# Wider weight transfers (2 MB, 14 to 16 KB rows) in a decode kernel: sliding-window attention with a gated FFN

## Chip, cores and metric

The kernel runs on one core of a Trainium2 chip. The metric is device time in microseconds (us), lower is better. Each execution reports its time and the mean clock that was granted to the TensorE. All runs counted here are fast: none lies more than 1.5% above the fastest of its kernel. In the profile PE is the TensorE matmul, PEld its weight load, DVE the VectorE, ACT the ScalarE, POOL the GpSimd, and SP the SyncE; an SPq entry is SP's sequencer, here the one that issues almost all DMAs.

## The reference

One decode step for 8 sequences with model width 512. A layer norm feeds two branches. Branch A is attention with 32 query heads over 8 cached K/V heads, of which only the last 1024 positions count. Branch B is a gated FFN of width 1792. The result combines them.

```python
x  = A_x                                    # (8, 1, 512), all bf16
xn = layernorm(x)
# A: q = xn @ wq -> 32 heads of 128; window of the last 1024 of 4096 positions
#    o = softmax(q k^T / sqrt(128)) v ;  s = o @ wo
# B: g = silu((gelu(xn @ w_gate) * (xn @ w_up)) @ w_down)
return x + s * g
```

K and V in the window are 33.6 MB. The weights wq, wo (4.19 MB each), w_gate, w_up and w_down (1.84 MB each) are 13.9 MB. Everything is read once: 47.46 MB.

## The kernel before

SP issues all large loads in the order of use, as 1 MB tiles (128 partitions of 8 KB) into one ring of 21 slots: K of the first group, four tiles of wq, then K and V of 16 groups alternating, six FFN tiles, four tiles of wo.

```python
ring = ctx.enter_context(tc.tile_pool(name="ring", bufs=21))
small = ctx.enter_context(tc.tile_pool(name="small", bufs=3))
def slot():
    return ring.tile([P, SLOT], BF16, name="slot")        # SLOT = 4096 elements, 8 KB
def load_wq():
    for k in range(NDC):                                   # 4 transfers of 1 MB
        t = slot()
        nc.sync.dma_start(out=t, in_=A_wq[k * P : (k + 1) * P, :])
        wq_t.append(t)
# ... load_ffn: two transfers of 896 KB, 7 KB rows, for each of gate, up, down
HS = SLOT // D                                             # 8 sub-rows of wo per partition
NM = Hq // HS                                              # 4 tiles of wo
def load_wo(m, cut=HS):
    t = slot().rearrange("p (e d) -> p e d", e=HS)
    src = A_wo[m * HS * Dh : (m + 1) * HS * Dh, :].rearrange("(p e) d -> p e d", e=HS)
    for lo, hi in ((0, cut), (cut, HS)):
        if lo < hi:
            nc.sync.dma_start(out=t[:, lo:hi, :], in_=src[:, lo:hi, :])
    wo_t[m] = t
# ...
for m in range(NM):
    load_wo(m, cut=HS if m < NM - 1 else HS - 2)           # last tile in two pieces
```

The output projection at the end is one group of matmuls per wo tile. A matmul waits for the transfer that brings the part it reads, so in the last tile 24 of the 32 matmuls wait for the piece of 6 sub-rows, and 8 wait for the last 2.

```python
def project_out(m):
    for e in range(HS):
        for q in range(NQ):                                # NQ = 4
            nc.tensor.matmul(s_ps[32 * q : 32 * q + B, :], oE[m][:, e, :],
                             wo_t[m][:, e, q * P : (q + 1) * P], ...)
# ... main loop over 64 blocks, then expand_out, ffn_up, select_out, ffn_down, then
for m in range(NM):
    project_out(m)
# tmp = s_ps * g ; out_sb = tmp + x ; four output writes, alternating SP and ACT
```

The softmax here doesn't subtract the row's maximum and nothing guards it: scores larger than these inputs give would overflow.

Of the kernel before, what the change touches and what calls it, by code (L numbers as in the profile page):

```python
# [10 lines left out]
BF16 = mybir.dt.bfloat16  # L11
# [4 lines left out]
def kernel(  # L16
# [13 lines left out]
    nc = tc.nc  # L30

    B, Sq, D = A_x.shape
# [5 lines left out]
    F = B_w_gate.shape[1]  # L38
    P = nc.NUM_PARTITIONS
    NDC = D // P  # L40
# [10 lines left out]
    CB = 8  # L51
    NB = C // CB
    SLOT = C * Dh

    JF = F // P
    NQ = D // P
# [3 lines left out]

    front = ctx.enter_context(tc.tile_pool(name="front", bufs=1))
    front.tile([P, 96], FP32, name="front_pad")
    ring = ctx.enter_context(tc.tile_pool(name="ring", bufs=21))
    consts = ctx.enter_context(tc.tile_pool(name="consts", bufs=1))
    persist = ctx.enter_context(tc.tile_pool(name="persist", bufs=1))
    kT_pool = ctx.enter_context(tc.tile_pool(name="kT_pool", bufs=4))
    p_pool = ctx.enter_context(tc.tile_pool(name="p_pool", bufs=3))
    small = ctx.enter_context(tc.tile_pool(name="small", bufs=3))
    ps_kT = ctx.enter_context(tc.tile_pool(name="ps_kT", bufs=3, space=bass.MemoryType.PSUM))
    ps_sc = ctx.enter_context(tc.tile_pool(name="ps_sc", bufs=2, space=bass.MemoryType.PSUM))  # L70
    ps_m = ctx.enter_context(tc.tile_pool(name="ps_m", bufs=2, space=bass.MemoryType.PSUM))
# [9 lines left out]
    def slot():  # L81
        return ring.tile([P, SLOT], BF16, name="slot")

    k_t, v_t, wo_t = {}, {}, {}
    wq_t, wg_t, wu_t, wd_t = [], [], [], []

    def load_cache(src, g):
        t = slot()
        hkv, b0 = g // GPH, (g % GPH) * I
        rows = src[b0 : b0 + I, hkv, win0:Sk, :].rearrange("i (r c) d -> r i (c d)", c=C)  # L90
        nc.sync.dma_start(out=t, in_=rows)  # L91
        return t
# [4 lines left out]
    def load_v(g):  # L97
        v_t[g] = load_cache(A_v_cache, g)

    def load_wq():  # L100
        for k in range(NDC):
            t = slot()
            nc.sync.dma_start(out=t, in_=A_wq[k * P : (k + 1) * P, :])  # L103
            wq_t.append(t)

    def load_ffn():
        for dst, src in ((wg_t, B_w_gate), (wu_t, B_w_up)):
            for a in range(2):
                t = slot()
                nc.sync.dma_start(  # L110
                    out=t[:, 0 : 2 * F],
                    in_=src[a * 2 * P : (a + 1) * 2 * P, :].rearrange(
                        "(p k) f -> p (k f)", k=2
                    ),
                )
                dst.append(t[:, 0 : 2 * F].rearrange("p (k f) -> p k f", k=2))
        JH = JF // 2
        wd = B_w_down.rearrange("(p j) d -> p j d", j=JF)
        for a in range(2):
            t = slot()[:, 0 : JH * D].rearrange("p (j d) -> p j d", j=JH)  # L120
            nc.sync.dma_start(out=t, in_=wd[:, a * JH : (a + 1) * JH, :])
            wd_t.extend(t[:, j, :] for j in range(JH))


    HS = SLOT // D
    NM = Hq // HS
    DQ = Dh // HS

    def load_wo(m, cut=HS):
        t = slot().rearrange("p (e d) -> p e d", e=HS)  # L130
        src = A_wo[m * HS * Dh : (m + 1) * HS * Dh, :].rearrange("(p e) d -> p e d", e=HS)
        for lo, hi in ((0, cut), (cut, HS)):
            if lo < hi:
                nc.sync.dma_start(out=t[:, lo:hi, :], in_=src[:, lo:hi, :])
        wo_t[m] = t

    load_k(0)
    load_wq()
    for g in range(1, NG):
        load_k(g)  # L140
        load_v(g - 1)
    load_v(NG - 1)
    load_ffn()
    for m in range(NM):
        load_wo(m, cut=HS if m < NM - 1 else HS - 2)


    ident = consts.tile([P, P], BF16, name="ident")
    nc.vector.memset(ident, 0.0)
    nc.gpsimd.affine_select(  # L150
        out=ident, in_=ident, compare_op=ALU.not_equal, fill=1.0, base=0,
# [10 lines left out]
        out=sel, in_=sel, compare_op=ALU.not_equal, fill=1.0, base=0,  # L162
# [4 lines left out]
        out=diag, in_=sel.rearrange("p r i -> p i r"), axis=AX.X, op=ALU.add  # L167
    )
    nc.vector.tensor_scalar(
        out=diag, in0=diag, scalar1=1.0, scalar2=30000.0, op0=ALU.subtract, op1=ALU.mult  # L170
# [6 lines left out]
        out=hmask, in_=hmask, compare_op=ALU.is_ge, fill=0.0, base=0,  # L177
# [3 lines left out]
        out=hmask, in_=hmask, compare_op=ALU.is_ge, fill=0.0, base=B - 1,  # L181
# [5 lines left out]
        out=bsel3, in_=bsel3, compare_op=ALU.not_equal, fill=1.0, base=0,  # L187
# [4 lines left out]
        out=bsel_f, in_=bsel3.rearrange("p h b -> p b h"), axis=AX.X, op=ALU.add  # L192
# [7 lines left out]
    for q in range(NQ):  # L200
        nc.scalar.dma_start(
            out=xq_sb[32 * q : 32 * q + B, :], in_=x_flat[:, q * P : (q + 1) * P]
# [10 lines left out]
    xhat = persist.tile([B, D], BF16, name="xhat")  # L213
    nc.vector.tensor_scalar(  # L214
        out=xhat, in0=x_sb, scalar1=mv[:, 0:1], scalar2=rstd[:, 0:1],
# [14 lines left out]

    def transpose_x():
        t = ps_m.tile([P, 2, NDC, B], BF16, name="m_ps")
        for k in range(NDC):
            nc.tensor.transpose(t[:, 0, k, :], xhat[:, k * P : (k + 1) * P], ident[0:B, 0:B])  # L234
        xp = xhat.rearrange("b (a p k) -> b a k p", a=2, k=2)
        for a in range(2):
            for k in range(2):
                nc.tensor.transpose(t[:, 1, 2 * a + k, :], xp[:, a, k, :], ident[0:B, 0:B])
        nc.vector.tensor_copy(out=xnT_sb[:, :, 0:B], in_=t[:, 0])
        nc.vector.tensor_copy(out=xpT_sb[:, :, 0:B], in_=t[:, 1])  # L240

# [153 lines left out]

    def ffn_up():
        gu_ps = [ps_m.tile([P, JQ * P], FP32, name="m_ps") for w in range(2)]
        for w, wt in enumerate((wg_t, wu_t)):
            for k in range(NDC):
                cols = wt[k // 2][:, k % 2, :].rearrange("x (p j) -> x j p", j=JF)  # L400
                for q in range(NQ):
                    nc.tensor.matmul(  # L402
                        gu_ps[w][Q * q : Q * (q + 1), :],
                        xpT_sb[:, k, :],
                        cols[:, j0[q] : j0[q] + JQ, :],
                        start=(k == 0),
                        stop=(k == NDC - 1),
                        skip_group_check=True,
                    )
        shape = [P, JQ * P]  # L410
        zT, uT = gu_ps
        z2 = persist.tile(shape, FP32, name="z2")
        nc.scalar.activation(out=z2, in_=zT, func=ACT.Square)
        nc.vector.tensor_scalar(
            out=z2, in0=z2, scalar1=0.044715, scalar2=1.0, op0=ALU.mult, op1=ALU.add
        )
        nc.vector.tensor_tensor(out=z2, in0=z2, in1=zT, op=ALU.mult)
        th = persist.tile(shape, FP32, name="th")
        nc.scalar.activation(out=th, in_=z2, func=ACT.Tanh, scale=0.7978845608028654)
        nc.vector.tensor_scalar(  # L420
            out=th, in0=th, scalar1=0.5, scalar2=0.5, op0=ALU.mult, op1=ALU.add
        )
        nc.vector.tensor_tensor(out=z2, in0=th, in1=zT, op=ALU.mult)
        h_sb = persist.tile(shape, BF16, name="h_sb")
        nc.vector.tensor_tensor(out=h_sb, in0=z2, in1=uT, op=ALU.mult)
        h_ps = ps_m.tile([P, JQ, P], BF16, name="m_ps")
        for c in range(JQ):
            nc.tensor.transpose(h_ps[:, c, :], h_sb[:, c * P : (c + 1) * P], ident)
        nc.vector.tensor_copy(out=hT_sb, in_=h_ps)

    def ffn_down():
        f_ps = ps_m.tile([P, P], FP32, name="m_ps")
        nc.vector.memset(f_ps, 0.0)
        for j in range(JF):
            r = j // JQ
            for q in range(NQ):
                nc.tensor.matmul(
                    f_ps[Q * q : Q * q + B, :],
                    hT_sb[:, j - j0[r], Q * r : Q * r + B],
                    wd_t[j][:, q * P : (q + 1) * P],  # L440
                    start=(j == 0),
                    stop=(j == JF - 1),
                    skip_group_check=True,
                )
        th2 = persist.tile([P, P], FP32, name="th2")
        nc.scalar.activation(out=th2, in_=f_ps, func=ACT.Tanh, scale=0.5)
        nc.vector.tensor_scalar(
            out=th2, in0=th2, scalar1=0.5, scalar2=0.5, op0=ALU.mult, op1=ALU.add
        )
        nc.vector.tensor_tensor(out=g_sb, in0=th2, in1=f_ps, op=ALU.mult)  # L450


    LA, LAG = 2, 6
    N = NG * NB
    transpose_x()
    for n in range(LA):
        transpose_block(n)
    project_q()
    for n in range(N + LAG):
# [4 lines left out]
        if n >= LAG:  # L464
# [3 lines left out]
            if g % GM == 0 and g > 0:  # L468
                if s == 0:
                    expand_out(g // GM - 1)  # L470
                if s == 3:
                    select_out(g // GM - 1)
    expand_out(NM - 1)
    ffn_up()
    select_out(NM - 1)
    ffn_down()
    xr_sb = persist.tile([P, P], FP32, name="xr_sb")
    nc.vector.tensor_copy(out=xr_sb, in_=xq_sb)
# [7 lines left out]
    for q in range(NQ):  # L486
        eng = nc.sync if q % 2 == 0 else nc.scalar
        eng.dma_start(
            out=out_flat[:, q * P : (q + 1) * P], in_=out_sb[32 * q : 32 * q + B, :]
# [31 lines left out]
```

## Time and profile before

| | before |
|---|---|
| time, median | 123.18 us (123.18 to 123.19, 3 runs) |
| span of the profile | 121.1 us |
| bytes read from HBM | 47.46 MB |
| share of queue 1 in the 16 DMA engines' span | 93.7% |
| PE / DVE / ACT busy | 71% / 60% / 19% |

The first lines are from the page of the kernel before: the slices (40 equal parts of the span, each 3.03 us; the DMA digit is the busy share in tenths), the DMA queue, and the chain of work that ended last.

```profile
DMA  3999999999999999999999999999999999999820
GB/s 84 387 430 430 430 427 417 419 430 425 425 427 427 425 414 422 430 419 430 425 427 422 422 417 430 422 425 422 425 433 418 422 414 434 416 430 423 341 88 5
DMA packets 6929, 47.73 MB, mean 394 GB/s; under 512 B 888, under 2 KB 896, under 8 KB 1920
q1 hardware_dynamic: 6800, 47.46, 93.7%
DMA 82%; PE 12%; DVE 2%; SPq 1%; issue 0%
```

The DMA is busy from the second slice to the 37th, at about 425 GB/s. No other engine is near that. So the time is the time to move 47.46 MB, plus what comes before the first byte and after the last.

What comes after the last bytes is in the timeline of the kernel before (start, duration, engine, line, operation, operands, count; in brackets the idle time before it and what ended it).

```profile
109.96 1.02 PE L383 MATMUL s_ps<-slot,oE_1066 128*8 128x128 bf16 x32 [0.32 <-DMA slot<-in_A_wo_dram]
112.40 1.02 PE L383 MATMUL s_ps<-slot,oE_1569 128*8 128x128 bf16 x32 [1.42 <-DMA slot<-in_A_wo_dram]
114.84 1.02 PE L383 MATMUL s_ps<-slot,oE_2072 128*8 128x128 bf16 x32 [1.42 <-DMA slot<-in_A_wo_dram]
116.75 1.02 PE L383 MATMUL s_ps<-slot,oE_2360 128*8 128x128 bf16 x32 [0.88 <-DMA slot<-in_A_wo_dram]
117.82 0.29 DVE L483 TENSOR_TENSOR tmp<-s_ps,g_sb 128x128 f32<-128x128 f32 x1 [7.06 <-PE s_ps L383]
118.47 0.71 SPq L488 DMA_DIRECT2D out_dram<-out_sb  x2
```

The wo tiles land every 2.44 us per 1 MB, which is 430 GB/s. The last group starts when the 768 KB piece has landed, at 116.75 us, and its 32 matmuls take 1.02 us; the remaining 256 KB lands under them. Then come two small DVE operations and the output writes.

### The profile page before, as it was taken

How to read it: one execution, taken by the hardware profiler on the slowest of the kernel's cores; microseconds unless marked ns; L12 is line 12 of the kernel's file. 1: busy time of each engine (PE TensorE's matmuls, PEld its weight loads, DVE VectorE, ACT ScalarE, POOL GpSimd, SP SyncE). 2: the span in 40 equal slices, each digit the busy share in tenths (PEclk: the TensorE clock that was granted, in tenths of full speed). 3: DMA queues.
4: the chain of work that ended last, by engine and by line, in shares of the span. 5: the costliest groups of instructions: out<-in, count | busy, mean ns of one | idle time of the engine just before them, and what ended most of it. 6: DMA issues, size and time to landing. Idle time of an engine off the chain costs nothing.

```text
span 121.1 us, 4123 instructions
## 1 busy us (share of the span) xinstructions
PE 86.0 (71%) x1856; PEld 71.1 (59%) x1856; DVE 72.3 (60%) x150; ACT 22.6 (19%) x70; POOL 2.4 (2%) x15
## 2 busy tenths in 40 slices
PE   0075269696875968999997969566798789955450
PEld 0061029586865957999896969565698542134340
DVE  2352046866956749678989987747798670562000
ACT  0440000321303301212330330303033300300000
POOL 6100000000000000000000000000000000000000
PEclk9999756999999985559999999999999756995555
DMA  3999999999999999999999999999999999999820
GB/s 84 387 430 430 430 427 417 419 430 425 425 427 427 425 414 422 430 419 430 425 427 422 422 417 430 422 425 422 425 433 418 422 414 434 416 430 423 341 88 5
DMA packets 6929, 47.73 MB, mean 394 GB/s; under 512 B 888, under 2 KB 896, under 8 KB 1920
## 3 DMA queue, kind: packets, MB, share of 16 engines
q1 hardware_dynamic: 6800, 47.46, 93.7%
q8 instruction: 14, 0.23, 0.7%
q10 hardware_dynamic: 112, 0.02, 0.1%
q14 instruction: 3, 0.02, 0.1%
HBM read 47.46 MB, written 0.01 MB: 392 GB/s over the span
## 4 chain that ended last, share of the span: by engine, by line
DMA 82%; PE 12%; DVE 2%; SPq 1%; issue 0%
DMA slot<-in_A_k_cache_dram 44%; DMA slot<-in_B_w_gate_dram 16%; DMA slot<-in_A_wo_dram 15%; DMA slot<-in_A_wq_dram 7%; PE kT_ps L282 7%; PE m_ps L329 2%; PE sc_ps L294 2%; SPq L91 1%; PE s_ps L383 1%; DVE kT L286 1%; PE m_ps L316 1%; DVE sums L318 1%; SPq L103 0%; PE m_ps L370 0%; DVE tmp L483 0%
## 5 line engine op out<-in xcount | busy, mean ns | idle before, releaser
L286 DVE COPY kT<-kT_ps 128x1024 bf16<-128x1024 bf16 x64 | 42.2, 677 | 18.1 <-PE kT_ps L282 17.5
L282 PE MATMUL kT_ps<-ident,slot 128*128 128x128 bf16 x512 | 43.4, 234 | 9.9 <-DMA slot<-in_A_k_cache_dram 9.5
L282 PEld LDWEIGHTS <-slot 128*128 128x128 bf16 x512 | 32.6, 104 | 13.3 <-DMA slot<-in_A_k_cache_dram 10.1
L304 ACT ACTIVATE pT<-sc_ps,diag 128x128 bf16<-128x128 f32 x64 | 18.2, 368 | 70.6 <-PE sc_ps L294 70.6
L294 PE MATMUL sc_ps<-qT_all,kT 128*128 128x16 bf16 x512 | 22.9, 171 | 0.3 <-issue 0.3
L329 PE MATMUL m_ps<-pT,slot 128*128 128x16 bf16 x512 | 21.8, 170 | 1.2 <-issue 1.1
L329 PEld LDWEIGHTS <-slot 128*128 128x128 bf16 x512 | 18.6, 97 | 4.6 <-issue 3.1
L294 PEld LDWEIGHTS <-kT 128*128 128x128 bf16 x512 | 20.4, 99 | 0.0
L318 DVE TENSOR_REDUCE sums<-m_ps 128x16 f32<-128x512 f32 x16 | 10.9, 684 | 1.2 <-PE m_ps L316 1.2
L402 PE MATMUL m_ps<-slot,xpT_sb 128*32 128x512 bf16 x32 | 7.7, 1105 | 0.0
L316 PE MATMUL m_ps<-pT,ones_pp 128*128 128x512 bf16 x16 | 6.7, 416 | 0.7 <-ACT pT L304 0.7
L250 PE MATMUL m_ps<-slot,xnT_sb 128*32 128x512 bf16 x32 | 3.5, 527 | 4.2 <-DMA slot<-in_A_wq_dram 4.2
L234 PE MATMUL m_ps<-ident,xhat 8*128 8x8 bf16 x4 | 0.3, 168 | 7.0 <-DVE xhat L214 7.0
L259 DVE CAST q_sb<-m_ps 128x512 bf16<-128x512 f32 x2 | 1.3, 686 | 6.6 <-PE m_ps L250 6.6
L356 DVE TENSOR_TENSOR wide<-m_ps,hmask 64x1024 bf16<-64x1024 bf16 x4 | 4.9, 1216 | 0.5 <-PE m_ps L352 0.4
L483 DVE TENSOR_TENSOR tmp<-s_ps,g_sb 128x128 f32<-128x128 f32 x1 | 0.3, 292 | 7.1 <-PE s_ps L383 7.1
L250 PEld LDWEIGHTS <-xnT_sb 128*32 128x32 bf16 x32 | 0.8, 101 | 6.2 <-issue 5.8
L322 DVE RECIPROCAL recip<-sums 128x16 f32<-128x16 f32 x16 | 4.0, 253 | 0.6
L234 PEld LDWEIGHTS <-xhat 8*128 8x128 bf16 x4 | 0.2, 102 | 7.0 <-DVE xhat L214 7.0
L402 PEld LDWEIGHTS <-xpT_sb 128*32 128x32 bf16 x32 | 1.7, 117 | 4.3 <-issue 3.4
L338 DVE TENSOR_TENSOR oT_all<-m_ps,recip 128x16 bf16<-128x16 f32 x16 | 3.5, 218 | 0.4 <-PE m_ps L329 0.3
L352 PE MATMUL m_ps<-ident,oT_all 128*64 128x128 bf16 x4 | 1.0, 253 | 2.7 <-DVE sums L318 2.1
(71 smaller groups left out, 33.4 us busy)
## 6 DMA issues: line engine op xcount, KB each, us to landing
slot<-in_A_k_cache_dram SPq DMA_DIRECT2D x16, 1024.0 KB, 19.4
slot<-in_A_v_cache_dram SPq DMA_DIRECT2D x16, 1024.0 KB, 19.7
slot<-in_A_wq_dram SPq DMA_DIRECT2D x4, 1024.0 KB, 8.6
slot<-in_A_wo_dram SPq DMA_DIRECT2D x3, 1024.0 KB, 18.0
slot<-in_B_w_gate_dram SPq DMA_DIRECT2D x2, 896.0 KB, 20.0
slot<-in_B_w_up_dram SPq DMA_DIRECT2D x2, 896.0 KB, 18.9
slot<-in_B_w_down_dram SPq DMA_DIRECT2D x2, 896.0 KB
slot<-in_A_wo_dram SPq DMA_DIRECT2D x1, 768.0 KB, 17.7
```

The costliest lines, as they stand in the source:

```text
L250: nc.tensor.matmul(q_ps[n][Q * q : Q * (q + 1), :], xnT_sb[:, k, :], wq_t[k][:, hkv * NW : (hkv + 1) * NW], start=(k == 0), stop=(k == NDC ...
L282: nc.tensor.transpose(t_ps[:, c * P : (c + 1) * P], k_t[g][:, cc * Dh : (cc + 1) * Dh], ident)
L286: nc.vector.tensor_copy(out=kT[n], in_=t_ps)
L294: nc.tensor.matmul(sc[g][:, s * CB + c, :], kT[n][:, c * P : (c + 1) * P], qT_all[:, hkv, b0 : b0 + I, :], start=True, stop=True,)
L304: nc.scalar.activation(out=pT[g][:, :, i * rep : (i + 1) * rep], in_=sc[g][:, :, i * rep : (i + 1) * rep], func=ACT.Exp, bias=diag[:, i : ...
L316: nc.tensor.matmul(sums_ps, ones_pp, pT[g], start=True, stop=True)
L318: nc.vector.tensor_reduce(out=sums, in_=sums_ps.rearrange("p c m -> p m c"), axis=AX.X, op=ALU.add)
L322: nc.vector.reciprocal(out=recip[g], in_=sums)
L329: nc.tensor.matmul(oT[g], v_t[g][:, c * Dh : (c + 1) * Dh], pT[g][:, c, :], start=(c == 0), stop=(c == C - 1),)
L338: nc.vector.tensor_tensor(out=oT_all[:, hkv * rep : (hkv + 1) * rep, b0 : b0 + I].rearrange("p j i -> p i j"), in0=oT[g].rearrange("p (i j ...
L356: nc.vector.tensor_tensor(out=wide, in0=t_ps.rearrange("p (q e) -> p e q", e=HS) .unsqueeze(2) .to_broadcast([HS * B, HS, HS, DQ]), in1=hm ...
L402: nc.tensor.matmul(gu_ps[w][Q * q : Q * (q + 1), :], xpT_sb[:, k, :], cols[:, j0[q] : j0[q] + JQ, :], start=(k == 0), stop=(k == NDC - 1), ...
```

## The change

The intent is fewer and larger transfers with longer rows for the weights. A second ring of 4 slots of 16 KB takes wq (two 2 MB tiles), gate, up and down (one transfer each, 14 KB rows) and wo (two 2 MB tiles). The K/V ring gives up 8 slots of 8 KB for it, and `small` one buffer.

```diff
+    WSLOT = 2 * SLOT
-    ring = ctx.enter_context(tc.tile_pool(name="ring", bufs=21))
+    ring = ctx.enter_context(tc.tile_pool(name="ring", bufs=13))
+    wide_ring = ctx.enter_context(tc.tile_pool(name="wide_ring", bufs=4))
-    small = ctx.enter_context(tc.tile_pool(name="small", bufs=3))
+    small = ctx.enter_context(tc.tile_pool(name="small", bufs=2))
     def load_wq():
-        for k in range(NDC):
-            t = slot()
-            nc.sync.dma_start(out=t, in_=A_wq[k * P : (k + 1) * P, :])
-            wq_t.append(t)
+        for a in range(2):
+            t = wide_slot()
+            src = A_wq[a * 2 * P : (a + 1) * 2 * P, :].rearrange("(p k) n -> p (k n)", k=2)
+            nc.sync.dma_start(out=t, in_=src)
+            t = t.rearrange("p (k n) -> p k n", k=2)
+            wq_t.extend(t[:, k, :] for k in range(2))
     def load_ffn():
-        # ... (two transfers for each of the three)
+        for src, k in ((B_w_gate, NDC), (B_w_up, NDC), (B_w_down, JF)):
+            n = src.shape[0] * src.shape[1] // P
+            t = wide_slot()[:, 0:n]
+            nc.sync.dma_start(out=t, in_=src.rearrange("(p k) f -> p (k f)", k=k))
+            ffn_t.append(t.rearrange("p (k f) -> p k f", k=k))
-    HS = SLOT // D
+    HS = WSLOT // D
     def load_wo(m, cut=HS):
-        t = slot().rearrange("p (e d) -> p e d", e=HS)
+        t = wide_slot().rearrange("p (e d) -> p e d", e=HS)
     # ... the two layouts of the transposed x follow the new row order
```

HS goes from 8 to 16, so there are two groups of the output projection, of 64 matmuls each, and two expansions of 128x2048 on DVE in place of four of 64x1024. The cut of the last wo tile stays `HS - 2`, now 14 and 2 sub-rows.

More of the change, by code (lines that the diff above doesn't have):

```diff
@@ L82, in slot, with wide_slot @@
         return ring.tile([P, SLOT], BF16, name="slot")
+    def wide_slot():
+        return wide_ring.tile([P, WSLOT], BF16, name="wide_slot")
     k_t, v_t, wo_t = {}, {}, {}
-    wq_t, wg_t, wu_t, wd_t = [], [], [], []
+    wq_t, ffn_t = [], []
     def load_cache(src, g):
@@ L100, in load_wq @@
     def load_wq():
-        for k in range(NDC):
-            t = slot()
-            nc.sync.dma_start(out=t, in_=A_wq[k * P : (k + 1) * P, :])
-            wq_t.append(t)
-    def load_ffn():
-        for dst, src in ((wg_t, B_w_gate), (wu_t, B_w_up)):
-            for a in range(2):
-                t = slot()
-                nc.sync.dma_start(
-                    out=t[:, 0 : 2 * F],
-                    in_=src[a * 2 * P : (a + 1) * 2 * P, :].rearrange(
-                        "(p k) f -> p (k f)", k=2
-                    ),
-                )
-                dst.append(t[:, 0 : 2 * F].rearrange("p (k f) -> p k f", k=2))
-        JH = JF // 2
-        wd = B_w_down.rearrange("(p j) d -> p j d", j=JF)
-        for a in range(2):
-            t = slot()[:, 0 : JH * D].rearrange("p (j d) -> p j d", j=JH)
-            nc.sync.dma_start(out=t, in_=wd[:, a * JH : (a + 1) * JH, :])
-            wd_t.extend(t[:, j, :] for j in range(JH))
-    HS = SLOT // D
+        for a in range(2):
[4 more added lines that the diff above has]
+            wq_t.extend(t[:, k, :] for k in range(2))
+    def load_ffn():
+        for src, k in ((B_w_gate, NDC), (B_w_up, NDC), (B_w_down, JF)):
[4 more added lines that the diff above has]
+    HS = WSLOT // D
     NM = Hq // HS
@@ L232, in transpose_x @@
         t = ps_m.tile([P, 2, NDC, B], BF16, name="m_ps")
+        xn = xhat.rearrange("b (a p k) -> b a k p", a=2, k=2)
+        xp = xhat.rearrange("b (p k) -> b k p", k=NDC)
         for k in range(NDC):
-            nc.tensor.transpose(t[:, 0, k, :], xhat[:, k * P : (k + 1) * P], ident[0:B, 0:B])
-        xp = xhat.rearrange("b (a p k) -> b a k p", a=2, k=2)
-        for a in range(2):
-            for k in range(2):
-                nc.tensor.transpose(t[:, 1, 2 * a + k, :], xp[:, a, k, :], ident[0:B, 0:B])
+            nc.tensor.transpose(t[:, 0, k, :], xn[:, k // 2, k % 2, :], ident[0:B, 0:B])
+        for k in range(NDC):
+            nc.tensor.transpose(t[:, 1, k, :], xp[:, k, :], ident[0:B, 0:B])
         nc.vector.tensor_copy(out=xnT_sb[:, :, 0:B], in_=t[:, 0])
@@ L397, in ffn_up @@
         gu_ps = [ps_m.tile([P, JQ * P], FP32, name="m_ps") for w in range(2)]
-        for w, wt in enumerate((wg_t, wu_t)):
+        for w, wt in enumerate(ffn_t[0:2]):
             for k in range(NDC):
-                cols = wt[k // 2][:, k % 2, :].rearrange("x (p j) -> x j p", j=JF)
+                cols = wt[:, k, :].rearrange("x (p j) -> x j p", j=JF)
                 for q in range(NQ):
@@ L439, in ffn_down @@
                     hT_sb[:, j - j0[r], Q * r : Q * r + B],
-                    wd_t[j][:, q * P : (q + 1) * P],
+                    ffn_t[2][:, j, q * P : (q + 1) * P],
                     start=(j == 0),
```

## The prediction

> **What bounds the kernel now.** The DMA. The page's queue table gives queue 1 a 93.7% share of the 16 engines' span; the 40-slice table shows DMA at 9 tenths from 3 us to 112 us, mostly at 414 to 434 GB/s; the chain that ended last is 82% DMA and 12% PE. 47.46 MB must be read. In the timeline the four wo pieces release their matmuls at 109.96, 112.40, 114.84 and 116.75 us: 2.44 us per 1 MB, or 430 GB/s. The Trainium skill ("DMA: Bandwidth & Descriptors", "Where 436 GB/s comes from") puts the ceiling at 435.2 GB/s; the trace agrees: no slice exceeds 434. The weights already run within about 1% of that.
>
> **What the change can gain.** wq, wo and the FFN weights are 13.9 MB, about 32.4 us of transfer. The skill's section "Why small descriptors are slow" charges about 3 cycles per packet beside one cycle per 32 B; an estimate from that for 16 KB instead of 8 KB rows is 0.6%, so 0.2 us. Fewer issues save nothing: SP waits for landings, not for issue (0.53 us each).
>
> **What it moves.**
> - Ring of 13 instead of 21. The DMA runs about 8 transfers ahead (19.6 us from issue to landing). V of group g and K of group g+2 come free near that group's normalisation on DVE. Those times (28.6, 33.3, ..., 51.0, 56.4 us) beside the issue times of the K loads 13 tiles later (34.2, 39.4, ..., 54.0, 58.9 us) leave at least 2.5 us, with 8 MB still queued. Cost: 0.
> - Wide ring of 4. The second wo load reuses the gate slot, so it waits until the gate matmuls end, near 102.7 us; the queue before it lasts to 112.4 us. Cost: 0.
> - q projection: about 1 us more matmul work after wq's last landing. PE still idles 1.4 us for K at 24.5 us. Cost: 0.
> - FFN: gate lands whole at about 98.9, up at about 103.1 us; ffn_up ends about 0.5 us later than 106.4. That is hidden before wo.
> - HS goes from 8 to 16: two expansions of 128x2048 instead of four of 64x1024; estimated 2.3 us each against 1.22. Absorbed by the slack above.
> - The tail. The last wo piece is still split, with 256 KB last. Before, 24 of 32 matmuls start when the 768 KB part lands (116.75 us); all finish 1.02 us later. After, 56 of 64 matmuls wait for a 1.75 MB part that ends at the same byte count. 32 more matmuls at 1.02/32 us follow the last big landing: **+1.0 us, all of it on the critical path**.
>
> **Sum.** 123.18 - 0.2 + 1.0 = 124.0 us, range 122.9 to 125.0. Faster by over 2%: 0.03; within 2%: 0.92; slower: 0.05.
>
> **What would show each step.** Weight stage still 2.40 to 2.44 us per MB. No long SP waits for PE at the K and V loads, DMA at 9 tenths throughout. Last group of wo matmuls x64, about 2.04 us (1.02 before), starting at 116.3 to 116.8 us. PE share of the chain up, DMA share down.
>
> **What would make it wrong.** 16 KB rows moving faster or slower by more than 1%; the K and V stage shifting by itself; the smaller ring letting the queue run dry while the PE clock is low; a different granted clock in the tail, where it is now 0.5; the second wo load waiting longer for the gate slot.

## The result, and the profile after

The changed kernel takes 123.77 us (median of 4 runs, 123.56 to 123.82), the kernel before in the same rounds 123.18 us (123.16 to 123.19). The ratio is 1.0045, with a 95% interval from 1.0027 to 1.0062: within 2%, and slower by about half a per cent. Ratios here are the mean time of one kernel's fast runs over that of the other's in the same rounds, so they are not quite the ratio of the medians.

The same parts of the page, for the changed kernel:

```profile
DMA  3999999999999999999999999999999999999600
GB/s 70 428 426 432 401 430 430 428 425 428 422 430 419 428 414 425 411 430 419 428 425 428 428 425 422 425 417 425 430 426 440 424 433 419 436 421 430 257 27 3
DMA packets 5920, 47.72 MB, mean 392 GB/s; under 512 B 776, under 2 KB 784, under 8 KB 912
q1 hardware_dynamic: 5792, 47.45, 92.7%
DMA 84%; PE 11%; SPq 1%; DVE 0%; issue 0%
```

Queue 1 moves the same bytes in 1008 fewer packets. A packet of a load is one row of it, 128 for each transfer, and each transfer has 16 small packets besides: 7 transfers fewer make 896 rows and 112 small packets fewer. The DMA is busy in the same slices. (A slice is 3.05 us here and was 3.03 us, so the 38th, 257 against 341 GB/s, is not the same stretch of time; the landings in the timeline are the better measure.) And its timeline at the end:

```profile
98.92 3.82 PE L400 MATMUL m_ps<-wide_slot,xpT_sb 128*32 128x512 bf16 x16 [1.27 <-DMA wide_slot<-in_B_w_gate_dram]
102.78 1.41 SPq L132 DMA_DIRECT2D wide_slot<-in_A_wo_dram  x2
103.07 3.83 PE L400 MATMUL m_ps<-wide_slot,xpT_sb 128*32 128x512 bf16 x16 [0.34 <-DMA wide_slot<-in_B_w_up_dram]
112.24 1.88 PE L381 MATMUL s_ps<-wide_slot,oE 128*8 128x128 bf16 x64 [2.23 <-DMA wide_slot<-in_A_wo_dram]
116.48 1.88 PE L381 MATMUL s_ps<-wide_slot,oE 128*8 128x128 bf16 x64 [2.37 <-DMA wide_slot<-in_A_wo_dram]
118.41 0.29 DVE L481 TENSOR_TENSOR tmp<-s_ps,g_sb 128x128 f32<-128x128 f32 x1 [7.28 <-PE s_ps L381]
119.05 0.71 SPq L486 DMA_DIRECT2D out_dram<-out_sb  x2
```

Read the two timelines against each other. The last large piece of wo lands 0.27 us sooner (116.48 against 116.75 us). Most of that arises in the FFN and wo stage: by the trace's landing times the thirteenth of the 16 V loads was only 0.04 us ahead (82.07 against 82.11 us). The group behind it takes 1.88 us instead of 1.02, so 0.86 us more. The DVE operation after it starts 0.59 us later, and the output writes are issued 0.58 us later. From the first output write to the end of the span the trace has 2.67 us before and 2.81 us after, another 0.14 us. In sum the span grows by 0.73 us. The time of these two profiled executions grows by 0.49 us only (123.24 and 123.73): the part of the time that lies outside the span is 2.1 us in the one and 1.9 us in the other. In all profiled runs it lies between 1.7 and 2.15 us and I found no rule in it. So I compare positions in the trace and not times of single kernels, which agree to about 0.2 us only. How far positions repeat can be seen from three profiles with the same end (after, after_again and ring7): the last wo group starts at 116.48, 116.50 and 116.48 us. The kernel before has a single profile.

### The profile page after: what moved, and what is told of

Same layout as the page of the kernel before. It is cut to its first block, busy times and chain, and to the rows that moved or that the text cites. A ratio compares the mean times of both kernels' runs of the same rounds, so it can differ in the third digit from the quotient of the medians.

```text
span 121.9 us, 4103 instructions
## 1 busy us (share of the span) xinstructions
PE 83.1 (68%) x1854; PEld 68.6 (56%) x1854; DVE 71.9 (59%) x146; ACT 22.6 (19%) x70; POOL 2.6 (2%) x15
## 4 chain that ended last, share of the span: by engine, by line
DMA 84%; PE 11%; SPq 1%; DVE 0%; issue 0%
DMA slot<-in_A_k_cache_dram 30%; DMA wide_slot<-in_B_w_gate_dram 18%; DMA slot<-in_A_v_cache_dram 17%; DMA wide_slot<-in_A_wo_dram 11%; DMA wide_slot<-in_A_wq_dram 8%; PE kT_ps L280 4%; PE m_ps L400 3%; PE s_ps L381 2%; SPq L96 1%; PE sc_ps L292 1%; PE m_ps L327 1%; PE m_ps L314 1%; DVE tmp L481 0%; DVE out_sb L483 0%
## 5 line engine op out<-in xcount | busy, mean ns | idle before, releaser
L280 PE MATMUL kT_ps<-ident,slot 128*128 128x128 bf16 x512 | 41.9, 229 | 12.7 <-DMA slot<-in_A_k_cache_dram 12.7
L280 PEld LDWEIGHTS <-slot 128*128 128x128 bf16 x512 | 31.7, 102 | 14.6 <-DMA slot<-in_A_k_cache_dram 13.6
L327 PEld LDWEIGHTS <-slot 128*128 128x128 bf16 x512 | 18.3, 96 | 3.1 <-issue 1.4
L400 PE MATMUL m_ps<-wide_slot,xpT_sb 128*32 128x512 bf16 x32 | 7.6, 1087 | 1.6 <-DMA wide_slot<-in_B_w_gate_dram 1.3
L381 PE MATMUL s_ps<-wide_slot,oE 128*8 128x128 bf16 x128 | 3.8, 310 | 4.6 <-DMA wide_slot<-in_A_wo_dram 4.6
L248 PE MATMUL m_ps<-wide_slot,xnT_sb 128*32 128x512 bf16 x32 | 3.8, 626 | 4.5 <-DMA wide_slot<-in_A_wq_dram 4.5
L314 PE MATMUL m_ps<-pT,ones_pp 128*128 128x512 bf16 x16 | 6.2, 389 | 0.7 <-ACT pT L302 0.7
L381 PEld LDWEIGHTS <-oE 128*8 128x8 bf16 x128 | 3.4, 124 | 4.9 <-issue 4.9
L354 DVE TENSOR_TENSOR wide<-m_ps,hmask 128x2048 bf16<-128x2048 bf16 x2 | 4.6, 2292 | 0.3 <-PE m_ps L350 0.3
L400 PEld LDWEIGHTS <-xpT_sb 128*32 128x32 bf16 x32 | 0.8, 110 | 6.7 <-issue 4.5
## 6 DMA issues: line engine op xcount, KB each, us to landing
slot<-in_A_k_cache_dram SPq DMA_DIRECT2D x16, 1024.0 KB, 19.6
```

What stands on the lines that cost most here:

```text
L248: nc.tensor.matmul(q_ps[n][Q * q : Q * (q + 1), :], xnT_sb[:, k, :], wq_t[k][:, hkv * NW : (hkv + 1) * NW], start=(k == 0), stop=(k == NDC ...
L280: nc.tensor.transpose(t_ps[:, c * P : (c + 1) * P], k_t[g][:, cc * Dh : (cc + 1) * Dh], ident)
L314: nc.tensor.matmul(sums_ps, ones_pp, pT[g], start=True, stop=True)
L327: nc.tensor.matmul(oT[g], v_t[g][:, c * Dh : (c + 1) * Dh], pT[g][:, c, :], start=(c == 0), stop=(c == C - 1),)
L354: nc.vector.tensor_tensor(out=wide, in0=t_ps.rearrange("p (q e) -> p e q", e=HS) .unsqueeze(2) .to_broadcast([HS * B, HS, HS, DQ]), in1=hm ...
L400: nc.tensor.matmul(gu_ps[w][Q * q : Q * (q + 1), :], xpT_sb[:, k, :], cols[:, j0[q] : j0[q] + JQ, :], start=(k == 0), stop=(k == NDC - 1), ...
```

## The experiments

The theory is: the change gains about 0.27 us because longer rows need fewer packets, and loses 0.86 us because 64 instead of 32 matmuls wait for the last large piece of wo; rings, whole-tile waits in the FFN and the wider expansions cost nothing. The rivals are that the loss comes from the smaller K/V ring or from the FFN tiles that now arrive whole, and that the gain is the lower number of transfers, or chance.

All kernels below gave correct results. Three calls of four kernels were made, each on one chip with its own runs of the kernel before. The medians of the kernel before were 123.23, 123.19 and 123.19 us, the single runs between 122.99 and 123.40.

| kernel | median us (range) | ratio to before (95%) |
|---|---|---|
| wo_8_6_2 | 122.96 (122.80 to 123.12) | 0.9981 (0.9969 to 0.9994) |
| wo_16 | 124.22 (124.01 to 124.39) | 1.0082 (1.0068 to 1.0095) |
| wo_narrow | 123.54 (123.40 to 123.64) | 1.0026 (1.0014 to 1.0039) |
| wo_fine | 122.89 (122.67 to 123.13) | 0.9976 (0.9963 to 0.9988) |
| after_again (the changed kernel) | 123.75 (123.63 to 123.82) | 1.0044 (1.0032 to 1.0057) |
| two_8k | 123.89 (123.69 to 124.04) | 1.0054 (1.0042 to 1.0067) |
| gap_8k | 124.08 (124.01 to 124.25) | 1.0074 (1.0060 to 1.0087) |
| gap_4k | 124.83 (124.81 to 125.05) | 1.0137 (1.0123 to 1.0151) |
| ring7 | 123.69 (123.55 to 123.87) | 1.0045 (1.0032 to 1.0057) |
| narrow_plus5 | 124.31 (124.12 to 125.88) | 1.0138 (1.0089 to 1.0187) |
| fine_plus4 | 122.59 (122.49 to 122.64) | 0.9952 (0.9941 to 0.9964) |
| before_fine_plus6 | 125.49 (125.38 to 125.57) | 1.0188 (1.0175 to 1.0201) |

### The tail: wo_8_6_2 and wo_16

The edit changes only how the last 2 MB of wo are cut; `load_wo` takes a list of pieces.

```diff
-        load_wo(m, cut=HS if m < NM - 1 else HS - 2)
+        load_wo(m, cuts=(HS,) if m < NM - 1 else (8, 6, 2))     # wo_8_6_2
+        load_wo(m)                                               # wo_16: one piece, 16
```

> The changed kernel with the last 2 MB of wo in three pieces, 8, 6 and 2 of its 16 sub-rows, instead of 14 and 2. Tail theory (the loss is the 32 more matmuls behind the last big landing): the group that follows the last big landing is x32 again, 1.0 us, and the time falls by 0.86 us to about 122.9 us, 0.2% under before. Rival (the loss comes from the smaller ring, the whole-tile waits of the FFN or the rows): the time stays near 123.8 us.

> The changed kernel with the last 2 MB of wo in one piece, not cut. Tail theory: all 64 matmuls wait for the last byte, which lands 256 KB or 0.6 us later than the 14 of 16 sub-rows do now: about 124.4 us. Rival (the tail is not what counts): near 123.8 us.

The timeline of wo_8_6_2 at the end:

```profile
114.83 1.02 PE L382 MATMUL s_ps<-wide_slot,oE 128*8 128x128 bf16 x32 [0.57 <-DMA wide_slot<-in_A_wo_dram]
116.62 1.02 PE L382 MATMUL s_ps<-wide_slot,oE 128*8 128x128 bf16 x32 [0.77 <-DMA wide_slot<-in_A_wo_dram]
117.70 0.29 DVE L482 TENSOR_TENSOR tmp<-s_ps,g_sb 128x128 f32<-128x128 f32 x1 [6.33 <-PE s_ps L382]
```

and of wo_16:

```profile
116.94 1.88 PE L381 MATMUL s_ps<-wide_slot,oE 128*8 128x128 bf16 x64 [2.95 <-DMA wide_slot<-in_A_wo_dram]
118.87 0.29 DVE L481 TENSOR_TENSOR tmp<-s_ps,g_sb 128x128 f32<-128x128 f32 x1 [7.92 <-PE s_ps L381]
```

With the 1 MB piece in front, half of the matmuls run before the last large landing, the last group is x32 and 1.02 us again, and the kernel falls by about 0.8 us to 122.96 us, the expected 122.9. Without a cut, all 64 matmuls wait for the last byte, 0.46 us later than in the changed kernel, and the time rises by about 0.5 us. The expectation was 124.4; the last 256 KB cost 0.46 us instead of 0.6, because the uncut tile is complete at 116.90 us and the cut one only at 117.05. The rivals expected 123.8 us in both cases and fall as the cause of the loss: rings and FFN are the same in these two kernels as in the changed one.

### Only wo undone: wo_narrow

```diff
-    HS = WSLOT // D
+    HS = SLOT // D
-        t = wide_slot().rearrange("p (e d) -> p e d", e=HS)
+        t = slot().rearrange("p (e d) -> p e d", e=HS)
```

> The changed kernel with wo put back into the 8 KB slots (four 1 MB tiles, HS 8, last one cut 6 and 2); wq and the FFN weights stay in wide slots. Tail theory: the 0.86 us come back, and about two thirds of the 0.27 us gain stay, since 9.7 of 13.9 MB keep the long rows: about 123.0 us. Rival (ring of 13, or the whole FFN tiles, cost the time): near 123.8 us.

The time is 123.54 us, half a microsecond over the expectation, and so this run looks like support for the rival. The timeline says otherwise:

```profile
116.49 1.02 PE L381 MATMUL s_ps<-slot,oE 128*8 128x128 bf16 x32 [1.23 <-DMA slot<-in_A_wo_dram]
117.56 0.29 DVE L481 TENSOR_TENSOR tmp<-s_ps,g_sb 128x128 f32<-128x128 f32 x1 [4.55 <-PE s_ps L381]
118.20 0.71 SPq L486 DMA_DIRECT2D out_dram<-out_sb  x2
```

The output writes are issued at 118.20 us, 0.85 us sooner than in the changed kernel and 0.27 us sooner than in the kernel before, as the tail theory has it. (The landing at 116.49 us is as early as with wo in wide slots, although 256 of the 896 saved rows are back; the expectation had 0.09 us of the gain lost by that. Differences of this size are not resolved here.) The gain is lost after that: from the first output write to the end of the span it takes 3.22 us, against 2.81 after and 2.67 before. This was not in my prediction, and it needed a theory of its own (below).

### Finer pieces: wo_fine

The edit is the one of wo_8_6_2 with pieces of 8, 4, 2, 1 and 1 sub-rows.

> The changed kernel with the last 2 MB of wo in pieces of 8, 4, 2, 1 and 1 sub-rows. Tail theory: after the last byte (about 117.1 us in the profile) only 4 matmuls are left, so the end comes about 1.0 to 1.1 us sooner than in the changed kernel: 122.7 us. If three more small transfers slow the end of the DMA, the time is no better than the 122.9 us expected of the 8, 6, 2 cut.

```profile
114.75 1.03 PE L382 MATMUL s_ps<-wide_slot,oE 128*8 128x128 bf16 x32 [0.57 <-DMA wide_slot<-in_A_wo_dram]
115.95 1.60 PE L382 MATMUL s_ps<-wide_slot,oE 128*8 128x128 bf16 x32 [0.18 <-DMA wide_slot<-in_A_wo_dram]
117.60 0.29 DVE L482 TENSOR_TENSOR tmp<-s_ps,g_sb 128x128 f32<-128x128 f32 x1 [6.38 <-PE s_ps L382]
```

The time, 122.89 us, misses the expected 122.7 and is not clear of wo_8_6_2. The last 32 matmuls now start as their pieces arrive, spread over 1.60 us, and the DVE operation starts 0.10 us sooner than with 8, 6, 2. The last four start at 117.27 us, just after the last piece has landed (117.23): once the matmuls keep up with the pieces, the wait is for the last bytes themselves. These land 0.18 us later than in the changed kernel (117.05), and the closing part is 0.11 us longer (2.92 against 2.81 us), and both work against the expectation.

### Row length: after_again, two_8k, gap_8k and gap_4k

Three kernels shorten the rows of the wide tiles again, two of them to 8 or 7 KB and one to 4 KB and less, with slots and matmuls as in the change. The first splits each transfer in two. The second keeps one transfer per tile, and puts a gap of 64 bytes into the middle of the slot so that no write can be longer than half a row; the third has four parts (seven for w_down). The last wo tile, with its 14 and 2 cut, is left alone in all three.

```diff
# two_8k (wq shown; FFN and the first wo tile alike)
-            nc.sync.dma_start(out=t, in_=src)
+            for h in range(2):
+                half = slice(h * SLOT, (h + 1) * SLOT)
+                nc.sync.dma_start(out=t[:, half], in_=src[:, half])
# gap_8k: PAD = 32 elements, h = 2 parts (gap_4k: 4)
+    def gapped(t, h, n):
+        c = (WSLOT + PAD * 2) // h
+        return t[:, 0 : c * h].rearrange("p (h c) -> p h c", h=h)[:, :, 0:n]
-            nc.sync.dma_start(out=t, in_=src)
+            t = gapped(t, 2, WSLOT // 2)
+            nc.sync.dma_start(out=t, in_=src.rearrange("p (h n) -> p h n", h=2))
```

> The changed kernel unaltered, as the yardstick for the three row experiments on the same chip: 123.77 us, 1.0045 of before; last big wo landing near 116.5 us in the profile.

> The changed kernel, but every wide tile except the last wo tile is loaded in two transfers of 8 or 7 KB rows (6 more transfers); slots and matmuls as in the change. If the 0.27 us earlier landing comes from longer rows or fewer transfers, it is lost: last big wo landing near 116.7 us and about 124.0 us. If it comes from anything else (order, rings, chance): 123.8 us.

> The changed kernel, but the wide slots have a gap of 64 bytes in the middle, so that the same single transfer per tile has to write 8 or 7 KB rows (the last wo tile excepted). Row length theory: 124.0 us, as with two transfers. Number of transfers theory: 123.8 us, as in the changed kernel.

> As the 8 KB gap kernel, with four parts of 4 or 3.5 KB (w_down seven parts of 2 KB). Row length theory with a fixed cost per packet: the cost of halving doubles at each step, so 0.5 us or more over the 16 KB rows, 124.3 to 124.5 us. Number of transfers theory: 123.8 us.

The queue line of the page (packets, MB, share of the 16 engines' span) for after_again, gap_8k and gap_4k in this order:

```profile
q1 hardware_dynamic: 5792, 47.45, 92.7%
```

```profile
q1 hardware_dynamic: 6560, 47.45, 92.7%
```

```profile
q1 hardware_dynamic: 8480, 47.45, 93.2%
```

and the last wo group in the timeline of the same three:

```profile
116.50 1.88 PE L381 MATMUL s_ps<-wide_slot,oE 128*8 128x128 bf16 x64 [2.38 <-DMA wide_slot<-in_A_wo_dram]
```

```profile
116.77 1.88 PE L401 MATMUL s_ps<-wide_slot,oE 128*8 128x128 bf16 x64 [2.36 <-DMA wide_slot<-in_A_wo_dram]
```

```profile
117.69 1.88 PE L401 MATMUL s_ps<-wide_slot,oE 128*8 128x128 bf16 x64 [2.35 <-DMA wide_slot<-in_A_wo_dram]
```

With the same number of transfers, 768 more packets put the last landing 0.27 us later, as much as the change had gained, and the median rises by 0.33 us. With 2688 more packets the landing is 1.19 us later and the median 1.08 us higher, above the expected 124.3 to 124.5 us (the expectation let the cost double at each halving of the rows; here there are 3.5 times as many additional packets). The number of transfers is the same in all three, so it cannot be the cause of these differences. Worked out per packet and engine, this is 0.27 us x 16 / 768 = 5.6 ns and 1.19 us x 16 / 2688 = 7.1 ns; the change itself gives 0.27 us x 16 / 1008 = 4.3 ns. In gap_4k the delay grows with the packets along the way: against after_again the gate matmuls start 0.48 us later (1152 more rows by then), the up matmuls 0.74 (1536) and the first wo group 1.22 (all 2688). So the cost goes with the packets. Its size at 8 KB is known less well: an error of 0.05 us in a landing is 1 ns per packet there, and the gaps may have a part in it.

two_8k has rows as short and six more transfers. In its profile the last landing is at 116.88 us, 0.38 us late, but its median is only 0.14 us above the changed kernel, with overlapping ranges; the profiled execution is the slowest of its five. The direction fits, but without the gaps the loss is not clear of the noise, so the row theory rests on the gap kernels. That the lower number of transfers gives part of the gain is not excluded.

### The K/V ring: ring7

```diff
-    ring = ctx.enter_context(tc.tile_pool(name="ring", bufs=13))
+    ring = ctx.enter_context(tc.tile_pool(name="ring", bufs=7))
```

> The changed kernel with the K/V ring at 7 slots instead of 13. Slack theory (the queue stays fed as long as some MB are in flight; 13 slots have room to spare): the issue of K and V now waits for PE, the time from issue to landing falls from 19.6 to between 7 and 12 us, and the time stays within 0.3 us of 123.77 us. Rival (the prefetch depth matters, so 13 slots must already cost something): over 1 us slower, with DMA slices under 9 tenths in mid kernel.

The SP waits of ring7 for the PE at the K and V loads (us in total, times, longest):

```profile
SPq L96 <- PE m_ps L327: 43.0, 11, 5.7
...
SPq L96 <- PE kT_ps L280: 11.3, 4, 5.4
```

and two DMA issue lines from its page (the last number is the median time in us from issue to landing):

```profile
slot<-in_A_k_cache_dram SPq DMA_DIRECT2D x16, 1024.0 KB, 11.3
slot<-in_A_v_cache_dram SPq DMA_DIRECT2D x16, 1024.0 KB, 13.5
```

Now SP does wait for the PE, for 54 us in all, and transfers are issued much later: 11 to 14 us before they land instead of 19.6. The time does not move (123.69 us), and the last wo group starts at 116.48 us as in the changed kernel. So even half of the changed ring is enough.

What SP waits for with 13 slots is in two lines of its waits in the changed kernel:

```profile
SPq L96 <- DMA slot<-in_A_k_cache_dram: 24.2, 13, 2.6
SPq L96 <- DMA slot<-in_A_v_cache_dram: 22.0, 11, 3.2
```

The program has eight semaphores for its DMAs and uses them in turn, so a load is issued when the DMA eight places before it has landed: the V load issued at 61.32 us takes the semaphore of one that landed at 61.26. Eight loads of about 2.44 us are the 19.6 us from issue to landing. The turn of eight and not the ring sets how far ahead the loads run, with 21 slots and with 13. In the changed kernel itself SP waits for the PE at the K and V loads for 0.8 us in all, and the K load that had the least room in the prediction is issued at 58.88 us against 58.86 before.

### The end of the program: narrow_plus5, fine_plus4 and before_fine_plus6

The kernel uses eight semaphores for its DMAs in turn. At the end of the program SP waits on all eight in a fixed order. The trace's records show these checks, in us counted from the first output write; here are three kernels, with the number of DMAs that each issues and the semaphore of the output write that is issued last:

```
before     56 DMAs, last write on 108: 103 +0.75  104 +0.81  105 +1.26  106 +1.44  107 +1.64  108 +1.84
after      49 DMAs, last write on  99: 103 +0.76  104 +0.82  105 +0.89  106 +1.88  107 +1.94  108 +2.00
wo_narrow  51 DMAs, last write on 103: 103 +1.82  104 +1.88  105 +1.95  106 +2.01  107 +2.07  108 +2.13
```

(The check of 104 also covers 101 and that of 105 also covers 99. A check of two appears to be recorded once its first semaphore has passed: in the changed kernel the record at 105 and 99 stands at +0.89, and the next one follows only at +1.88, about when the last write arrives in the other two.) Where the last output write uses the semaphore that is checked last, nothing is left to do when it arrives. Where it uses the one checked first, five more checks follow, 0.06 us each. Which one it is depends on the number of DMAs modulo 8: of the numbers that occur here, 56 and 48 give the best case, 51 the worst. The part from the first output write to the end of the span is 2.67 us for the kernels with 0 modulo 8 (before, wo_16), 2.81 to 2.82 us for those with 1 (after, after_again, gap_8k, gap_4k), 2.88 for 2, 3.22 for 3, 2.92 us for 4 and 2.85 for 7 (two_8k). ring7, with 1, has 2.97, which the order of the checks does not explain.

To test this, unused small loads were added to bring the number to a multiple of 8.

```diff
+    for i in range(5):            # narrow_plus5; 4 in fine_plus4, 6 in before_fine_plus6
+        spare = persist.tile([B, P], BF16, name=f"spare{i}")
+        nc.scalar.dma_start(out=spare, in_=x_flat[:, 0:P])
```

> wo_narrow with five unused 2 KB loads of x added on the ACT queue at the start, so that it issues 56 DMAs like the kernel before instead of 51. Theory of the closing waits (SP ends the program by waiting on the eight DMA semaphores in a fixed order, and the number of DMAs modulo 8 decides which of them the four output writes use): from the first output write to the end 2.67 us as in before, not 3.22 us, and the time falls by 0.4 to 0.5 us to about 123.1 us. Rival (wo_narrow's missing gain is lost elsewhere, or chance): 123.5 us, closing part near 3.2 us.

> wo_fine with four such unused loads, 56 DMAs instead of 52. Closing waits theory: closing part 2.67 instead of 2.92 us, about 122.65 us, the best of all. Rival: 122.9 us, as wo_fine.

> The kernel before with its last 1 MB of wo in pieces of 4, 2, 1 and 1 sub-rows and six unused loads (64 DMAs, also 0 modulo 8). It has the same short tail and closing part as fine_plus4 and differs from it by the rows and rings of the change. Row length theory: 0.2 to 0.3 us slower than fine_plus4, about 122.9 us. If the change gains nothing by its rows: equal to fine_plus4.

fine_plus4 does what was expected. Its output writes are issued at 118.23 us and those of wo_fine at 118.24 us, so the end of the work before them did not move (at the start the spare loads held up the second K load to 9.94 us from 2.58, but the queue did not run dry); the closing part is 2.67 instead of 2.92 us, and the time is 122.59 instead of 122.89 us. It beats both the kernel before (ratio 0.9952) and the changed kernel (1.0045 in the first rounds).

narrow_plus5 is a failed control with half an answer. The last of the eight checks is made at +1.85 us instead of +2.13, as before has it, so the order of the checks is confirmed. But the closing part is 2.94 us, not 2.67: after the checks the barrier between the engines takes 1.10 us, as in wo_narrow (1.09), and not 0.83 as in before. In both, the last DRAIN instruction of SP stands 0.64 us after the one before it, against 0.25 us in before; why is open. And the kernel is slower in all (four runs near 124.3 us, two near 125.8), because the spare loads hurt the start. Two lines from the SP waits of narrow_plus5 show it:

```profile
SPq L96 <- DMA xq_sb<-in_A_x_dram: 8.0, 1, 8.0
SPq L96 <- DMA wide_slot<-in_A_wq_dram: 4.6, 1, 4.6
```

The spare loads take semaphores in the same turn of eight. The second K load, issued at 2.59 us in the changed kernel, now waits until 10.58 us, the first V load until 15.77 us, and the queue runs low: the slices around 15 to 21 us show 374 and 346 GB/s where there were 430. In before_fine_plus6 it runs dry. Its slices:

```profile
DMA  3999499999999999999999999999999999999920
GB/s 80 390 422 429 106 422 425 430 417 430 425 435 425 422 417 427 425 419 427 419 427 419 425 419 430 417 430 422 430 425 415 427 419 430 420 430 422 360 105 5
```

One slice at 106 GB/s is about 2.3 us lost ((430 - 106) / 430 of 3.09 us), and the kernel comes out at 125.49 us. It cannot tell whether the kernel before with a finer tail would be level with fine_plus4, which was its purpose. That comparison stays open, and with it a test of the rows without gaps.

## Why the prediction was right

The predicted time was 124.0 us (122.9 to 125.0), the measured one 123.77 us. The terms:

- *What bounds the kernel.* Right: DMA at 9 tenths in the same slices in both profiles, and every change that moved the last landings moved the time.
- *Gain 0.2 us from longer rows.* Measured 0.27 us in the position of the last large landing, and as much is lost again when the rows are shortened by gaps (gap_8k). The estimate came from the Trainium skill's page "DMA: Bandwidth & Descriptors", section "Why small descriptors are slow" (about 3 cycles per packet). A cost per packet, as that section says, is what gap_4k shows; where in the DMA it arises no run shows. It measured 4.3 ns per packet and engine for the change itself and 5.6 and 7.1 ns in the gap kernels, against an estimate of about 3.5 ns for 3 cycles at the 850 MHz that the page gives for the fabric.
- *Ring of 13: cost 0.* Right, with more to spare than I reckoned: 7 slots cost nothing either. That the eight semaphores set the "about 8 transfers ahead" was not in the prediction.
- *Wide ring of 4: the second wo load waits until about 102.7 us, cost 0.* It was issued at 102.78 us, and the DMA stayed at 9 tenths up to slice 37.
- *q projection and FFN: later, but hidden.* The up matmuls end at 106.90 us instead of 106.39, the predicted half microsecond, and wo is awaited after that for over 2 us.
- *Expansions of 2.3 us each.* 2.29 us each in the trace, without effect on the end.
- *Tail +1.0 us.* Right in kind, 0.86 us in size. The term was 32 more matmuls at 1.02/32 us. Two points of the same line (32 in 1.02 us, 64 in 1.88 us, both at a granted clock of 0.5) give 27 ns for each further matmul and 0.16 us that a group takes once. I had spread the fixed part over the matmuls and counted it twice.
- *Not in the prediction:* 0.14 us more in the closing waits, because 49 DMAs instead of 56 put the last output write on a semaphore that is checked sooner.
- *PE share of the chain up, DMA share down.* Wrong as a sign: the chain went from 82% to 84% DMA and from 12% to 11% PE although the PE tail grew. The chain also picks a way through the middle of the kernel, where waits that end together are put down to one or the other, and that outweighs 0.86 us at the end. The timeline of the last groups was the better place to look.

In sum: -0.27 + 0.86 + 0.14 = +0.73 us of span, of which the timed executions show 0.49 (the profiled pair) and 0.59 us (the medians). The difference lies outside the span and was not explained.

That the number came so close is in part luck: the tail was put 0.14 us too high, the 0.14 us of the closing part were left out, and the two cancel. The predicted range also holds the time of the kernel before, so the time alone says little for the mechanism. What shows it are the wo experiments.

## What to carry to other kernels

When a kernel already streams at about 430 GB/s, there is little to gain from longer rows (here about 0.3 us, for rows doubled from 7 or 8 KB in 13.9 of 47 MB); what counted here is how much work waits for the last bytes. Larger tiles made that tail longer until the last tile was cut so that each piece is consumed while the next one lands: pieces of 8, 6 and 2 sub-rows turned +0.5% into -0.2%. Changing the number of DMAs also moves the end of the program by some tenths of a microsecond and can starve the start, so differences of that size are to be read from positions in the timeline, not from two times.

## What the Trainium skill lacked or had wrong

- "DMA: Bandwidth & Descriptors", section "Why small descriptors are slow", gives about 3 cycles per packet (about 3.5 ns at 850 MHz), shown there for 256 B. At rows of 2 to 16 KB these runs show 7.1 ns per packet and engine for 2688 more packets and 5.6 ns for 768, where the rows were shortened by gaps in the SBUF tile, so part of it could belong to the gap. The change itself, without gaps, comes to 4.3 ns for 1008 packets, which is too near to 3.5 ns to call the page wrong.
- The same page, section "Where 436 GB/s comes from", gives 435.2 GB/s as the ceiling of the fabric. The last large landing agrees (1.75 MB between the two last wo landings after, 4.24 us, is 433 GB/s), but single 3 us slices of the profile read up to 440 GB/s after and 455 GB/s in wo_fine, so a slice is not exact enough to judge the last per cent.
- I found on no page that the waits at the end of the program go over the DMA semaphores in a fixed order: 2.67 us from the first output write to the end with 56 DMAs, 3.22 us with 51, of which 0.29 us are the order of the checks.
- I found on no page that a program whose DMAs take eight semaphores in turn has no more than eight in flight, so that small DMAs hold up later large ones: with six unused 2 KB loads one slice fell to 106 GB/s and the kernel lost about 2.3 us.
